# The opening of a fused attention kernel: query part before later keys, and a new planned order

## The chip, the cores and the metric

The kernel runs on one core of a Trainium2 chip. The metric is the device time of one execution in microseconds (us), the median of several; lower is better. Before the change it is 843.43 us, the median of 3 runs (843.15 to 843.75).

## The reference

Three layers run one after the other. Cut to what matters:

```python
# q, k, v: [4, 8, 1152, 64]; w_in [512, 2048], w_out [2048, 512]
q_pool = q.reshape(B, H, S // 2, 2, D).mean(axis=3)          # 576 queries per head
scores = scale * q_pool @ k.T
attn = exp(scores - scores.max(-1)); attn /= attn.sum(-1) + 1e-9
x = (attn @ v).transpose(0, 2, 1, 3).reshape(2304, 512)
h = x @ w_in;  x = (h * cos(h)) @ w_out
# then eight small experts, fed and read through softmax weights of x @ phi
```

## The kernel before, in words

The attention takes the 32 heads two at a time: 16 pairs, which the code numbers `p`, and which the change's title calls units. Two heads of 64 rows share the 128 partitions. A pair has two halves `c` of 288 queries each, and each half has nine steps `t`, one for each 128 keys.

The softmax needs each row's maximum before the exponentials. It is found by a cheap first pass in bfloat16: a **round** (`round_`, L346) multiplies two blocks of 64 queries with 384 keys, and VectorE takes the maximum of each row (`reduce`, L349). A pair has 14 rounds, 8 for the first five query blocks and 6 for the other four. When the rounds of a group are reduced, TensorE turns the maxima (`by_head`, L356), VectorE takes the maximum over keys (`top`, L363 and L368), and ScalarE and VectorE write diagonal matrices `D` with the negated maxima (L382, L380).

A **step** then is: the scores in float32 (L463, L450), the subtraction of the maximum as one more product with `D` (L472), the exponential on ScalarE (L477), and the product with the values (L485). Rounds and scores share three banks of PSUM (`BANKS = 3`): a round gives its bank back when it is reduced, a score when its exponential is done. The exponentials are also added up, on VectorE, on GpSimd, and some by a DMA that adds into memory and is issued from GpSimd (L495, L497, L500); `ADD0` and `ADD1` hold one letter for each step of a half that says who adds it, a small letter for the DMA.

Nothing orders these operations by hand. `Plan` holds every operation with an estimated duration and a due time, simulates the engines' queues with these estimates, and writes the instructions in the order in which the simulation started them. The due times come from tables (`ROUNDS`, `FIRST_ROUNDS`, `DUES`) and the step length `P`. The tables set nothing but the order; on the chip each engine runs its instructions in that order and waits for semaphores.

The opening is special. For the first pair the queries come in three parts of 128, 192 and 256 columns, two rows of which are added into one (L284), the keys in three parts of 384; each part is also cast to bfloat16 (L287). While TensorE would idle, 16 **warm** products (L419, four matmuls each) run into a bank that nobody reads. The load of the first values (L277) is held back by a copy of one element on ScalarE (L271).

After the attention come the two large matmuls (L905), whose weights are decoded from 64-bit words by VectorE, ScalarE and GpSimd (L832 to L869, eight parts of them during the attention), and at the end the experts.

Of the kernel before, what the change touches and what calls it, by code (L numbers as in the profile page):

```python
# [25 lines left out]
class Plan:  # L26
# [3 lines left out]
    HOP = 0.08  # L30
    TAIL = {"P": 0.17, "A": 0.1, "V": 0.085, "G": 0.04}

# [5 lines left out]
    def op(self, due, eng, time, fn, after=(), new=(), uses=(), port=None, more=0.0, early=0.0, name=""):  # L38

        i = len(self.ops)
        for ring, size, key in new:
            self.sizes[ring], self.sizes_of[key] = size, ring
        for key in [k for _, _, k in new] + list(uses):
            self.users.setdefault(key, []).append(i)
        port = (eng == "G") if port is None else port
        self.ops.append((due, eng, time, fn, list(after), list(new), port, more, early, name))
        return i

    def order(self):
# [34 lines left out]
        for _ in range(len(ops)):  # L86
# [21 lines left out]
            for j in outs[i]:  # L108
                at[j] = max(at[j], free[eng] if eng == ops[j][1] == "P" else end[i] + self.HOP)
                left[j] -= 1  # L110
# [5 lines left out]
    def by_path(self, first, last, due, most):  # L116

        left = {last: 0.0}
        for i in range(last, first - 1, -1):
            if i in left:  # L120
# [4 lines left out]
                for d in o[4]:  # L125
                    p = self.ops[d]
                    wait = 0.0 if o[1] == p[1] == "P" else self.HOP + self.TAIL.get(p[1], 0.0) + p[7]
                    left[d] = max(left.get(d, 0.0), left[i] + wait)
# [7 lines left out]
class Attention:  # L136
# [7 lines left out]

    P = 1.277
    QB, KC = 64, 384

    FIRST_ADD0 = "VVvGGVVGG"  # L150
    FIRST_ADD1 = "VGVgVVGVG"
    FIRST_JOIN_BY = "G"
    ADD0 = "VVGvgVVGG"
    ADD1 = "VVgvVGVGG"

    ROUNDS = (-7.4, -5.0, -18.6, -10.7, -8.1, -10.2, -3.5, -2.9, -10.5, 8.1, 1.5, 8.0, -1.0, 9.4)
    FIRST_ROUNDS = (-90, -89, -88, -87, -86, -85, -84, -83, -65.3, -9.1, -12.9, 5.0, -3.2, 3.6)
    E_BUFS = 10
    XU, AG = 5, 3
    SINGLE = (15,)  # L160
    ISSUE, LANDING = 0.95, 5.5

    BEHIND = 28.96

    DUES = {
        "load": 9.4, "free": -20.1, "v": 32.8, "pooled": 21.9, "qb": -10.3, "kb": -18.8, "top": -82.8,
        "diagonal": 52.5, "add": 39.2, "whole": -54.1, "take": -45.0, "join": -44.3, "sums": 15.4, "out": 18.1,
        "fold": -30.9, "inv": -20.5, "row": 39.3, "spread": 11.1, "scale": -3.8, "high": 72.8, "low": 25.6,
        "delta": 13.2,
    }  # L170
    CHAIN, DELTA_BY = (0, 2, 4, 7, 8), "V"
    JOIN_BY, SCALE_BY, LOW_BY = "V", "G", "G"

    BANKS = 3

    AHEAD = 3

    WARM_FROM, WARM, WARM_EVERY = 8.6, 16, 0.34

# [58 lines left out]
    def operands(self, p, m):  # L238
        nc, op = self.nc, self.plan.op
        J, NQ, KC, NC, QB = self.J, self.NQ, self.KC, self.NC, self.QB  # L240
        S = J * 128
        q, k = self.q[2 * p:2 * p + 2].rearrange("h d (r s) -> (h d) r s", r=2), self.k[2 * p:2 * p + 2]
        k = k.rearrange("h d s -> (h d) s")
        at_ = lambda name, n=0.0: m + self.DUES[name] * self.P + n
        early = 0.0 if p == 0 else max(at_("free"), 9.0)
        at = lambda parts: [(sum(parts[:i]), n) for i, n in enumerate(parts)]
        q_parts = at([QB * 2, QB * (self.half - 2), NQ - QB * self.half] if p == 0 else [NQ])
        k_parts = at([KC] * NC if p == 0 else [S])

        def tiles():  # L250
            if p == 0:
                self.qr[p] = self.one.tile([128, 2, NQ], FP32, name="qr")
            self.kr[p] = self.three.tile([128, S], FP32, tag="kr", name="kr")
            self.mp[p] = self.three.tile([128, sum(len(x) for x in self.rounds), 2], FP32, tag="mp", name="mp")
            self.qs[p] = self.three.tile([128, NQ], FP32, tag="qs", name="qs")
            self.qb[p] = self.two.tile([128, NQ], BF16, tag="qb", name="qb")
            self.kb[p] = self.two.tile([128, S], BF16, tag="kb", name="kb")

        def load_q(a, n):
            if p:  # L260
                nc.sync.dma_start(out=self.qs[p][:, a:a + n], in_=q[:, 0, a:a + n])
            else:
                nc.sync.dma_start(out=self.qr[p][:, :, a:a + n], in_=q[:, :, a:a + n])

        def load_k(a, n):
            (nc.sync if p or a else nc.scalar).dma_start(out=self.kr[p][:, a:a + n], in_=k[:, a:a + n])

        def values():
            self.vr[p] = self.late.tile([128, 2, J, 64], FP32, tag="vr", name="vr")
            if p == 0:  # L270
                nc.scalar.copy(out=self.vr[p][:, 0, 0, 0:1], in_=self.qs[p][:, 2 * QB:2 * QB + 1])  # L271

        def load_v():
            if p:
                values()
            vr = self.vr[p]
            nc.sync.dma_start(out=vr, in_=self.v[2 * p:2 * p + 2].rearrange("h p (j d) -> p h j d", d=64))  # L277

        def pooled(a, n):
            if p:  # L280
                nc.gpsimd.dma_start(out=self.qs[p][:, a:a + n], in_=q[:, 1, a:a + n], accum_op=ALU.add)
                return
            qr, x = self.qr[p], slice(a, a + n)
            nc.vector.tensor_tensor(out=self.qs[p][:, x], in0=qr[:, 0, x], in1=qr[:, 1, x], op=ALU.add)  # L284

        def copy(dst, src, a, n):
            nc.scalar.copy(out=dst[p][:, a:a + n], in_=src[p][:, a:a + n])  # L287

        ring = lambda names, size: [(n, size, (n, p)) for n in names]
        new = ring(["kr", "qs", "mp"], 3) + ring(["qb", "kb"], 2)  # L290
        first = op(m, "SP", 0.0, tiles, new=new, early=early)
        self.q_after[p], self.k_after[p], self.s_after[p] = {}, {}, []
        late = 0.0
        for i, (a, n) in enumerate(q_parts):
            x = op(m + 0.5 * i, "SP", 0.6, lambda a=a, n=n: load_q(a, n), [first], uses=[("qs", p)],
                   more=4.2 if p else (3.0, 3.7, 3.9)[i], early=early)
            if p:
                x = op(at_("pooled"), "G", self.ISSUE, lambda a=a, n=n: pooled(a, n), [x], uses=[("qs", p)], port=False, more=self.LANDING)
            else:
                x = op(m + (-40.0, -40.0, 40.0)[i] * (p == 0), "V", 0.07 + n / 960, lambda a=a, n=n: pooled(a, n), [x], uses=[("qs", p)], port=True)  # L300
            self.s_after[p].append(x)
            self.last_q[p] = x
            c = op(at_("qb", 0.1 * i) if p else m + 1.0 + i, "A", 0.07 + n / 1180, lambda a=a, n=n: copy(self.qb, self.qs, a, n), [x],
                   uses=[("qs", p), ("qb", p)])
            for y in range(0, NQ, QB):
                if a <= y < a + n:
                    self.q_after[p][y // QB] = [c]
        for i, (a, n) in enumerate(k_parts):
            x = op(m + (0.1, 0.2, 0.3)[i], "A" if p == 0 and i == 0 else "SP", 0.6, lambda a=a, n=n: load_k(a, n), [first], uses=[("kr", p)],
                   more=5.6 if p else (2.8, 3.2, 3.4)[i], early=early)  # L310
            self.s_after[p].append(x)
            for y in range(a, a + n, KC):
                self.k_after[p][y // KC] = [op(at_("kb", 0.1 * i) if p else m + 1.1 + i + y / 1e4, "A", 0.405, lambda y=y: copy(self.kb, self.kr, y, KC), [x],
                                               uses=[("kr", p), ("kb", p)])]
        if p:
            n = 128 * (len(self.CHAIN) - 1)

            def delta():
                x = self.kr[p]
                self.engine(self.DELTA_BY).tensor_tensor(out=x[:, 0:n], in0=x[:, 0:n], in1=x[:, 128:128 + n], op=ALU.subtract)  # L320

            x = op(at_("delta"), self.DELTA_BY, (0.07 + n / 960, 0.08 + n / 447)[self.DELTA_BY == "G"], delta,
                   sum([x for x in self.k_after[p].values()], []), uses=[("kr", p)], port=True, name="delta")
            self.delta_after[p] = [x]
        new, uses, x = [("vr", 2, ("vr", p))], [], [self.v_after[p - 1]] if p else []
        if p == 0:
            x = [op(m + 2.5, "A", 0.1, values, self.q_after[0][2], new=new, uses=[("qs", p)])]
            new, uses = [], [("vr", p)]
        self.v_after[p] = op(at_("v"), "SP", 0.6, load_v, x, new=new, uses=uses, more=4.2, early=early + late)


    def maximum(self, p):
        nc, plan, P = self.nc, self.plan, self.P
        st, reds = {}, []
# [413 lines left out]
FIRST = [(i, f) for i in range(4) for f in range(2)]  # L748

FIRST_AT = 12.0  # L750
FIRST_FROM, FIRST_EVERY, FIRST_DUE = 0.53, -0.08, 1000
SEL_C = 4
URGENT = 14.0, 12.0

# [897 lines left out]
```

## Time and profile before

| | |
|---|---|
| median of the runs | 843.43 us |
| the profiled execution | 844.42 us, its span 842.6 us |
| TensorE busy | 828.3 us (98%) |
| VectorE busy | 700.7 us (83%) |
| ScalarE busy | 524.9 us (62%) |
| GpSimd busy | 388.9 us (46%) |
| granted TensorE clock, mean | 0.995 |

All durations below are those of the profiled execution. A row of the timeline names its start, its duration, the engine, the line of the code, the output and the input, how many instructions it merges, and in brackets the idle time before it with what ended it. The durations of matmuls overlap, so the time that one costs is read from the start of the next.

### The profile page before, as it was taken

How to read it: one execution, taken by the hardware profiler on the slowest of the kernel's cores; microseconds unless marked ns; L12 is line 12 of the kernel's file. 1: busy time of each engine (PE TensorE's matmuls, PEld its weight loads, DVE VectorE, ACT ScalarE, POOL GpSimd, SP SyncE). 2: the span in 40 equal slices, each digit the busy share in tenths (PEclk: the TensorE clock that was granted, in tenths of full speed). 3: DMA queues.
4: the chain of work that ended last, by engine and by line, in shares of the span. 5: the costliest groups of instructions: out<-in, count | busy, mean ns of one | idle time of the engine just before them, and what ended most of it. 6: DMA issues, size and time to landing. Idle time of an engine off the chain costs nothing.

```text
span 842.6 us, 23109 instructions
## 1 busy us (share of the span) xinstructions
PE 828.3 (98%) x9439; PEld 610.8 (72%) x9439; DVE 700.7 (83%) x1291; ACT 524.9 (62%) x1118; POOL 388.9 (46%) x398
## 2 busy tenths in 40 slices
PE   6999999999999999999999999999999999999996
PEld 3666666666666666668888888888888888877456
DVE  7899999999999999858999898989899989544523
ACT  4777777777777777766875555555555555454223
POOL 1567666666667666674544334344443333120100
PEclk9999999999999999999999999999999999999998
DMA  7246555555555554221211111111111110693997
GB/s 238 45 114 144 132 132 143 132 138 125 141 126 129 131 132 90 50 69 38 63 50 38 39 51 38 42 50 41 49 38 51 38 39 13 243 422 142 358 422 238
DMA packets 48347, 99.30 MB, mean 118 GB/s; under 512 B 12144, under 2 KB 20336, under 8 KB 44144
## 3 DMA queue, kind: packets, MB, share of 16 engines
q1 hardware_dynamic: 41616, 84.35, 30.8%
q0 software_dynamic: 6480, 13.27, 9.5%
q8 instruction: 74, 1.21, 0.6%
q14 instruction: 33, 0.27, 0.1%
q10 hardware_dynamic: 144, 0.20, 0.1%
HBM read 78.71 MB, written 4.72 MB: 99 GB/s over the span
## 4 chain that ended last, share of the span: by engine, by line
PE 96%; POOL 1%; DVE 1%; ACT 1%; DMA 0%; issue 0%; SPq 0%; ACTq 0%; POOLq 0%
PE hps L905 23%; PE ops L905 23%; PE o L485 16%; PE s L463 10%; PE s L450 7%; PE m L346 4%; PE s L472 2%; PE so L1517 2%; PE hq L1474 2%; PE xtp L1086 1%; PE sums L619 1%; PE fo L1546 1%; DVE mp L349 1%; PE lgp L1100 1%; PE sps L1285 1%; PE lg L1109 0%
## 5 line engine op out<-in xcount | busy, mean ns | idle before, releaser
L349 DVE TENSOR_REDUCE mp<-m 128x2 f32<-128x768 f32 x224 | 206.2, 951 | 18.4 <-PE m L346 16.6
L477 ACT ACTIVATE e<-s 128x576 f32<-128x576 f32 x288 | 174.0, 650 | 54.7 <-PE s L450 23.6
L905 PE MATMUL ops<-w,g 128*128 128x512 f32 x864 | 205.5, 391 | 0.0
L905 PE MATMUL hps<-x,w 128*128 128x512 f32 (+1 forms) x960 | 204.4, 368 | 0.0
L905 PEld LDWEIGHTS hps<-x,w 128*128 128x128 f32 x960 | 167.9, 188 | 32.1 <-issue 1.7
L905 PEld LDWEIGHTS ops<-w,g 128*128 128x128 f32 x864 | 160.8, 188 | 33.6 <-issue 0.8
L485 PE MATMUL o<-e,vr 64*64 64x288 f32 x2304 | 177.3, 403 | 0.0
L943 POOL TENSOR_TENSOR g<-r,g 128x512 fp32r<-128x512 f32 (+1 forms) x80 | 100.2, 1253 | 145.3 <-ACT g L940 119.3
L930 ACT ACTIVATE r<-r 128x512 f32<-128x512 f32 (+1 forms) x160 | 94.0, 587 | 69.7 <-DVE r L923 68.0
L463 PE MATMUL s<-qs,kr 64*64 64x288 f32 x1344 | 110.5, 408 | 1.4 <-PE m L346 0.8
L497 POOL TENSOR_TENSOR acc<-acc,e 128x576 f32<-128x576 f32 x64 | 92.1, 1439 | 30.8 <-ACT e L477 28.8
L485 PEld LDWEIGHTS o<-e,vr 64*64 64x64 f32 x2304 | 86.9, 133 | 26.0 <-issue 0.4
L866 POOL TENSOR_TENSOR da<-da,w 128x256 f32<-128x256 f32 x64 | 51.4, 803 | 97.8 <-DVE db L855 42.0
L346 PE MATMUL m<-kb,qb 64*64 64x384 bf16 x896 | 75.7, 330 | 6.2 <-ACT qb L287 4.2
L450 PE MATMUL s<-qs,kr 64*64 64x288 f32 x960 | 80.1, 403 | 0.0
L923 DVE SCALAR_TENSOR_TENSOR r<-ki,hps 128x512 f32<-128x512 int32 (+1 forms) x80 | 50.4, 629 | 34.0 <-ACT ki L920 32.0
L940 ACT CAST g<-r 128x512 fp32r<-128x512 f32 (+1 forms) x80 | 46.2, 577 | 39.1 <-DVE r L933 36.6
L463 PEld LDWEIGHTS s<-qs,kr 64*64 64x64 f32 x1344 | 46.4, 132 | 31.7 <-ACT e L477 8.0
L920 ACT ACTIVATE ki<-hps 128x512 int32<-128x512 f32 (+1 forms) x80 | 44.0, 549 | 36.4 <-PE hps L905 35.3
L1066 DVE TENSOR_TENSOR acc<-acc,ops 128x512 f32<-128x512 f32 x70 | 47.6, 684 | 22.1 <-PE ops L905 22.0
L495 POOL DMA_DIRECT2D acc<-e x30 | 26.0, 868 | 86.3 <-ACT e L477 86.3
L346 PEld LDWEIGHTS <-qb 64*64 64x64 bf16 x896 | 34.4, 107 | 28.8 <-issue 4.6
(162 smaller groups left out, 1094.6 us busy)
## 6 DMA issues: line engine op xcount, KB each, us to landing
raw<-in_w_io_dram SPq DMA_DIRECT2D x64, 256.0 KB
w1t<-in_w_dram SPq DMA_DIRECT2D x15, 1024.0 KB
vr<-in_v_dram SPq DMA_DIRECT2D x16, 576.0 KB
kr<-in_k_dram SPq DMA_DIRECT2D x15, 576.0 KB
acc<-e POOLq DMA_DIRECT2D x30, 288.0 KB, 4.4
w2t<-in_w2b_dram SPq DMA_DIRECT2D x8, 1024.0 KB
qs<-in_q_dram SPq DMA_DIRECT2D x15, 288.0 KB
qs<-in_q_dram POOLq DMA_DIRECT2D x15, 288.0 KB, 4.5
```

The lines of the kernel that those rows point to most:

```text
L346: nc.tensor.matmul(ps[heads[c], h.start // 64, 0:self.KC], w, m, start=True, stop=True)
L349: nc.vector.tensor_reduce(out=self.mp[p][:, x], in_=st[i][:, :, 0:self.KC], axis=AX.X, op=ALU.max)
L450: nc.tensor.matmul(out, w, self.qs[p][x, s], start=False, stop=True, skip_group_check=True)
L463: nc.tensor.matmul(ps[y:y + 64, h, 0:N], w, self.qs[p][x, s], start=True, stop=False)
L477: nc.scalar.activation(out=st["e"], in_=st["ps"][:, :, 0:N], func=ACTF.Exp, scale=1.0 / 16.0)
L485: nc.tensor.matmul(self.o[u][64 * h:64 * h + 64, r, 0:N], self.vr[p][x, h, block(t)], st["e"][x, h], start=(t == 0), stop=(t == J - 1),)
L497: self.engine(who).tensor_tensor(out=acc[who], in0=x, in1=st["e"], op=ALU.add)
L866: nc.gpsimd.tensor_tensor(out=st["a"], in0=st["a"], in1=fl(half(0)), op=ALU.subtract)
L905: nc.tensor.matmul(ps, x, y, start=(i == 0 and m == 0), stop=(i == n - 1 and m == 2))
L923: nc.vector.scalar_tensor_tensor(out=st["r"], in0=st["ki"], scalar=-c, in1=x, op0=ALU.mult, op1=ALU.add)
L930: nc.scalar.activation(out=st["r"], in_=st["r"], **kw)
L943: nc.gpsimd.tensor_tensor(out=g["l"][:, i], in0=st["r"], in1=fl(g["h"][:, i]), op=ALU.subtract)
```

## The change

The second part of the first pair's queries is loaded before the second and third parts of its keys; the third part is still loaded last. Its planned landing times are new. The third part's add on VectorE gets an earliest planned time, which puts it behind the first diagonals. The copy that holds back the values' load waits for the cast of the last keys too. Two steps of some halves change hands: from the third pair on, the DMA adds step 2 of a second half instead of step 3, and in the first halves of the first two pairs step 3 instead of step 2 (`ADD0` names other letters for the same adds). `AHEAD`, the number of scores that may stand before the diagonals, goes from 3 to 1. All due times are new.

```diff
-    P = 1.277
+    P = 1.282
-    FIRST_ADD0 = "VVvGGVVGG"
+    FIRST_ADD0 = "VVgvGVVGG"
-    ADD0 = "VVGvgVVGG"
-    ADD1 = "VVgvVGVGG"
+    ADD0 = "VVgvgVVGG"
+    ADD1 = "VVvgVgVGG"
...
-    FIRST_ROUNDS = (-90, -89, -88, -87, -86, -85, -84, -83, -65.3, -9.1, -12.9, 5.0, -3.2, 3.6)
+    FIRST_ROUNDS = (-90, -89, -88, -87, -86, -85, -84, -83, -56.3, 4.6, -13.0, -6.0, 3.8, 4.6)
...
-    AHEAD = 3
+    AHEAD = 1
...
-            x = op(m + 0.5 * i, "SP", 0.6, lambda a=a, n=n: load_q(a, n), [first], uses=[("qs", p)],
-                   more=4.2 if p else (3.0, 3.7, 3.9)[i], early=early)
+            x = op(m + (0.0, 0.05, 0.9)[i], "SP", 0.6 if p else 0.45, lambda a=a, n=n: load_q(a, n), [first], uses=[("qs", p)],
+                   more=4.2 if p else (3.0, 3.3, 4.0)[i], early=early)
...
-                x = op(m + (-40.0, -40.0, 40.0)[i] * (p == 0), "V", 0.07 + n / 960, lambda a=a, n=n: pooled(a, n), [x], uses=[("qs", p)], port=True)
+                x = op(m + (-40.0, -40.0, 40.0)[i] * (p == 0), "V", 0.07 + n / 960, lambda a=a, n=n: pooled(a, n), [x], uses=[("qs", p)], port=True, early=12.7 * (i == 2))
...
-            x = [op(m + 2.5, "A", 0.1, values, self.q_after[0][2], new=new, uses=[("qs", p)])]
+            x = [op(m + 5.0, "A", 0.1, values, self.q_after[0][2] + self.k_after[0][2], new=new, uses=[("qs", p)])]
...
-FIRST_FROM, FIRST_EVERY, FIRST_DUE = 0.53, -0.08, 1000
+FIRST_FROM, FIRST_EVERY, FIRST_DUE = 1.25, -0.46, 1000
```

Every engine has the same instructions as before, and behind the first few pairs they stand in the same order. What moves is the start. On the queue of the loads (SP), at the head of the program, `qr` is the raw queries, `kr` the keys and `vr` the values:

```order
 L263 DMA qr<-in_q_dram 128x2x128
+L263 DMA qr<-in_q_dram 128x2x192
 L266 DMA kr<-in_k_dram 128x384 x2
-L263 DMA qr<-in_q_dram 128x2x192
 L263 DMA qr<-in_q_dram 128x2x256
 L277 DMA vr<-in_v_dram 128x2x576
```

The second part of the queries has moved past the two loads of keys.

On VectorE, in the opening of the first pair, `qs<-qr` is the add of a query part, `mp<-m` the reduce of a round, `mc` the maximum over keys and `D` a diagonal:

```order
 L224 TENSOR_SCALAR a_minus<-ident 64x64 x2
 L284 TENSOR_TENSOR qs<-qr 128x128
-L349 TENSOR_REDUCE mp<-m 128x2 x2
 L284 TENSOR_TENSOR qs<-qr 128x192
-L349 TENSOR_REDUCE mp<-m 128x2
+L349 TENSOR_REDUCE mp<-m 128x2 x8
+L363 TENSOR_REDUCE mc<-m 128x2x2
+L368 TENSOR_REDUCE mc<-m 128x1
+L380 TENSOR_SCALAR D<-a_minus,mc 128x64 x2
 L284 TENSOR_TENSOR qs<-qr 128x256
-L349 TENSOR_REDUCE mp<-m 128x2 x6
-L363 TENSOR_REDUCE mc<-m 128x2x2
```

The second add now stands before the first reduce, the third behind the diagonals, and eight reduces instead of nine stand before the maximum over keys.

On GpSimd, in the second half of a later pair, the numbers tell exponentials apart: `e_1440` is step 3, which ScalarE computes before step 2, `e_1453`. Before:

```order
L281 DMA qs_1325<-in_q_dram 128x576
L495 DMA acc_1451<-e_1440 128x576
L497 TENSOR_TENSOR acc_1485<-e_1453,e_1465 128x576
L497 TENSOR_TENSOR acc_1485<-acc_1485,e_1520 128x576
L497 TENSOR_TENSOR acc_1485<-acc_1485,e_1570 128x576
```

Now:

```order
L281 DMA qs_1325<-in_q_dram 128x576
L495 DMA acc_1451<-e_1453 128x576
L497 TENSOR_TENSOR acc_1485<-e_1440,e_1465 128x576
L497 TENSOR_TENSOR acc_1485<-acc_1485,e_1520 128x576
L497 TENSOR_TENSOR acc_1485<-acc_1485,e_1570 128x576
```

The two exponentials have changed places; the order of the instructions is the same.

On TensorE the 16 warm products keep their number and change their places: before, 12 of them stand in front of the turning of the first maxima (L356) and 4 between it and the first subtraction (L472), with three rounds among those 4; now 9 stand in front and 7 between, with no round among them.

## Rows read from the trace of the kernel before

**Rows 1.** The page's chain that ended last, by engine.

```profile
PE 96%; POOL 1%; DVE 1%; ACT 1%; DMA 0%; issue 0%; SPq 0%; ACTq 0%; POOLq 0%
```

**Rows 2.** Windows: stretch, length, busy of five engines (instructions), clock, DMA share, GB/s.

```profile
10.00:20.00 10.00, 8.57 (x156) 5.30 (x155) 9.19 (x16) 4.00 (x10) 1.01 (x1) 1.00 1.00 327
100.00:200.00 100.00, 99.99 (x1884) 66.59 (x1880) 94.56 (x145) 77.26 (x171) 63.65 (x63) 1.00 0.55 132
```

**Rows 3.** Timeline of the queue of the loads: late query parts, first values.

```profile
2.59 1.22 SPq L263 DMA_DIRECT2D qr<-in_q_dram  x2
...
8.06 0.39 SPq L277 DMA_DIRECT2D vr<-in_v_dram  x1
```

**Rows 4.** Timeline of the opening, VectorE and ScalarE.

```profile
4.82 0.96 DVE L349 TENSOR_REDUCE mp<-m 128x2 f32<-128x768 f32 x1 [0.97 <-PE m L346]
...
5.19 1.09 ACT L287 CAST kb<-kr 128x384 bf16<-128x384 f32 x2 [1.01 <-DMA kr<-in_k_dram]
...
7.21 0.35 DVE L284 TENSOR_TENSOR qs<-qr 128x192 f32<-128x192 f32 x1
...
12.14 2.69 DVE L349 TENSOR_REDUCE mp<-m 128x2 f32<-128x768 f32 x3 [0.19 <-PE m L346]
```

**Rows 5.** Timeline of the opening, TensorE.

```profile
4.23 0.53 PE L346 MATMUL m<-kb,qb 64*64 64x384 bf16 x4 [4.23 <-ACT qb L287]
...
7.66 1.24 PE L463 MATMUL s<-qs,kr 64*64 64x288 f32 x8 [0.80 <-PE m L346]
...
8.65 0.90 PE L346 MATMUL m<-kb,qb 64*64 64x384 bf16 x8
...
9.29 0.90 PE L419 MATMUL o<-kb,qb 64*64 64x384 bf16 x8
```

**Rows 6.** Timeline around the turning of the maxima, first half and second half.

```profile
14.12 0.30 PE L356 MATMUL m<-mp,ident 64*64 64x8 f32 x8
...
14.75 0.16 DVE L363 TENSOR_REDUCE mc<-m 128x4 f32<-128x12 f32 x1
...
14.94 0.82 ACT L382 ACTIVATE D<-a_minus,mc 128x64 bf16<-128x64 f32 x3 [5.74 <-DVE mc L363]
...
22.52 0.24 PE L356 MATMUL m<-mp,ident 64*64 64x6 f32 x8
...
22.84 0.17 DVE L363 TENSOR_REDUCE mc<-m 128x4 f32<-128x12 f32 x1 [0.65 <-PE m L356]
```

**Rows 7.** Timeline of TensorE from the first subtraction on.

```profile
16.30 0.36 PE L346 MATMUL m<-kb,qb 64*64 64x384 bf16 x4 [0.57 <-DVE mp L349]
16.46 0.32 PE L472 MATMUL s<-D,a_ones 64*64 64x288 bf16 x4
17.17 0.72 PE L463 MATMUL s<-qs,kr 64*64 64x288 f32 x8 [0.39 <-DVE mp L349]
...
17.82 0.67 PE L463 MATMUL s<-qs,kr 64*64 64x288 f32 x8
...
19.04 0.67 PE L485 MATMUL o<-e,vr 64*64 64x288 f32 x8
```

**Rows 8.** Timeline of later pairs: exponentials, GpSimd's adds, and VectorE beside them.

```profile
95.81 2.96 ACT L477 ACTIVATE e<-s 128x576 f32<-128x576 f32 x5 [0.33 <-PE s L472]
...
98.50 0.86 POOL L495 DMA_DIRECT2D acc<-e  x1 [2.09 <-ACT e L477]
...
100.90 0.68 DVE L320 TENSOR_TENSOR kr<-kr 128x512 f32<-128x512 f32 x1
...
116.77 1.41 POOL L497 TENSOR_TENSOR acc<-acc,e 128x576 f32<-128x576 f32 x1
...
117.61 1.19 DVE L497 TENSOR_TENSOR acc<-acc,e 128x576 f32<-128x576 f32 x1
```

**Rows 9.** Timeline of TensorE: row sums of the first pair and of the fourth.

```profile
50.24 0.70 PE L619 MATMUL sums<-acc,a_ones 128*32 128x144 f32 x16
...
116.26 0.70 PE L619 MATMUL sums<-acc,a_ones 128*32 128x144 f32 x16
```

More of the change, by code (lines that the diff above doesn't have):

```diff
@@ L136 @@
 class Attention:
-    P = 1.277
+    P = 1.282
     QB, KC = 64, 384
-    FIRST_ADD0 = "VVvGGVVGG"
+    FIRST_ADD0 = "VVgvGVVGG"
     FIRST_ADD1 = "VGVgVVGVG"
     FIRST_JOIN_BY = "G"
-    ADD0 = "VVGvgVVGG"
-    ADD1 = "VVgvVGVGG"
-    ROUNDS = (-7.4, -5.0, -18.6, -10.7, -8.1, -10.2, -3.5, -2.9, -10.5, 8.1, 1.5, 8.0, -1.0, 9.4)
-    FIRST_ROUNDS = (-90, -89, -88, -87, -86, -85, -84, -83, -65.3, -9.1, -12.9, 5.0, -3.2, 3.6)
+    ADD0 = "VVgvgVVGG"
+    ADD1 = "VVvgVgVGG"
+    ROUNDS = (-8.3, -4.7, -20.1, -9.5, -8.3, -10.2, -3.6, -2.8, -10.1, 0.8, -0.0, 0.5, 7.4, 9.2)
+    FIRST_ROUNDS = (-90, -89, -88, -87, -86, -85, -84, -83, -56.3, 4.6, -13.0, -6.0, 3.8, 4.6)
     E_BUFS = 10
@@ L161 @@
     ISSUE, LANDING = 0.95, 5.5
-    BEHIND = 28.96
+    BEHIND = 28.21
     DUES = {
[L166 to L169, printed above, removed]
+        "load": 16.1, "free": -31.4, "v": 39.2, "pooled": 27.6, "qb": 2.7, "kb": -27.1, "top": -88.5,
+        "diagonal": 39.2, "add": 48.0, "whole": -54.3, "take": -58.3, "join": -53.6, "sums": 15.1, "out": 16.7,
+        "fold": -29.6, "inv": -41.6, "row": 24.2, "spread": 20.3, "scale": -5.7, "high": 74.6, "low": 36.3,
+        "delta": 20.0,
     }
@@ L308, in operands @@
         for i, (a, n) in enumerate(k_parts):
-            x = op(m + (0.1, 0.2, 0.3)[i], "A" if p == 0 and i == 0 else "SP", 0.6, lambda a=a, n=n: load_k(a, n), [first], uses=[("kr", p)],
-                   more=5.6 if p else (2.8, 3.2, 3.4)[i], early=early)
+            x = op(m + (0.1, 0.2, 0.3)[i], "A" if p == 0 and i == 0 else "SP", 0.6 if p else 0.45, lambda a=a, n=n: load_k(a, n), [first], uses=[("kr", p)],
+                   more=5.6 if p else (2.6, 3.4, 3.7)[i], early=early)
             self.s_after[p].append(x)
```

## The prediction

> **What bounds the kernel now.** I read the chain of waits first: it is TensorE for 96% of the span [rows 1]. The windows then say where TensorE is not full. In a hundred microseconds of the attention it is busy for 99.99 of 100 us, while VectorE has 94.56 [rows 2]. From the row sums of the first pair to those of the fourth there are 66.02 us, 22.0 us a pair [rows 9], and in that stretch TensorE is fed without gaps. In the opening it is not: from 10 to 20 us it is busy for 8.57 us [rows 2], and much of that is warm products and matmuls at half speed. So the end of the kernel moves by what the opening wins or loses, as long as TensorE stays full behind it. Both programs have the same products on TensorE before the first row sums at 50.24 us. So one question remains: how much of those 50 us TensorE spends on nothing useful.
>
> What ends last in the opening is VectorE's eight reduces, then the turning of the maxima (14.12 us), the diagonals and the first subtraction at 16.46 us [rows 6, 7]. That first subtraction, here called X, is the mark for which I work out a new time.
>
> **When the reduces run.** Before, the first reduce starts at 4.82 us and the second query part is added at 7.21 us only, so the rounds of blocks 2 to 4 come late [rows 4]; its load was issued with the third from 2.59 us on, behind the keys [rows 3]. Now it has the place of the second key part, which has the same 192 KB and landed for the cast at 5.19 us [rows 4]. I take 5.2 us for its landing, the row of the same size and place. Its bounds are 4.2 us (the first part is there by 3.6, since its round starts at 4.23 [rows 5] after an add and a cast; 192 KB at the 327 GB/s of [rows 2] are 0.6 us more) and 7.2 us, when the add ran before [rows 4]. Each microsecond above 6.1 would reach the end, as the next part shows; below, it is covered by TensorE. The add takes 0.35 us [rows 4] and now stands ahead of the first reduce, which starts at about 5.5 us, 0.7 us later than before. The cast of that part then ends near 5.9 us (under 0.5 us, the length of a cast of keys in [rows 4]), and a round's matmuls need 0.59 us until the reduce starts (4.23 to 4.82 [rows 4, 5]), so the second reduce starts at 6.5 us. From there they run back to back, 0.90 us each (2.69 us for three [rows 4]): the eighth ends at 6.5 + 6 x 0.9 + 0.96 = 12.9 us. Before, nine reduces ended at 12.14 + 2.69 = 14.83 us. On VectorE alone that is a gain of 1.9 us, of which 0.9 is the ninth reduce that now waits.
>
> **When TensorE is ready.** It must do, after the bank of the fourth reduce comes free (6.5 + 2 x 0.9 + 0.96 = 9.3 us), the seventh and the eighth round, nine warm products, and a score. In the rows of the opening such a group of four bfloat16 matmuls takes 0.32 us (8.65 to 9.29 for two) and a score 0.99 us (7.66 to 8.65) [rows 5]. Later they take 0.16 (16.30 to 16.46) and about half a microsecond [rows 7]. The granted-clock column reads 1.00 from 10 to 20 us [rows 2], but the spacing says that the opening runs at 1.2 GHz and goes to 2.4 GHz between those rows, after TensorE had been packed from 7.66 us on. Now it is packed later, from 9.3 us on. At half speed the list takes 11 x 0.32 + 0.99 = 4.5 us, and the turning starts at 13.8 us instead of 12.95. I take 13.8.
>
> The Trainium skill, "TensorE: Matmul & The Clock Gate", Part 1, says that the throttled state is the default, that activity releases it, and that the point of release shifts from run to run. The trace agrees with the first two: half speed in [rows 5], full speed in [rows 7]. No run here shows the third. By that rule a sparser opening would get its clock later, which speaks against this change; the rival below prices it.
>
> **From the turning to X.** Before, VectorE was in its ninth reduce when the maxima were turned. With VectorE free, the maximum over keys starts 0.32 us after the turning (22.52 to 22.84), the diagonals 0.19 us later (14.75 to 14.94) and take 0.82 us [rows 6]: X can start at 13.8 + 0.32 + 0.19 + 0.82 + 0.07 = 15.2 us. In front of it TensorE has seven warm products. At full speed they take 7 x 0.16 = 1.1 us and are hidden; at half speed 2.2 us, and X starts at 16.1. Before, X stood behind three rounds, of which the last waited 0.57 us for a bank [rows 7]; that wait is gone. So X moves from 16.46 to 15.2 us: **1.26 us gained**.
>
> **What is given back.** Before, 12 rounds were done when X started, now 8. TensorE still has to do the four: 4 x 0.16 = **0.65 us lost**. One score stands ahead of X in both orders, so `AHEAD` by itself costs nothing.
>
> Behind X, before, the next score waited for a bank: 17.17 - 16.46 - 0.12 = 0.59 us [rows 7]. Now that bank is free, but the six rounds of the second half all come behind X. The first can start 0.73 us after X (a subtraction and a step of 0.65, 17.17 to 17.82 [rows 7]); the next bank comes free with the first exponential, 0.2 us late. Six reduces and the keys' difference (0.68 [rows 8]) keep VectorE busy until about 1.15 + 5.4 + 0.7 = 7.3 us behind X, and TensorE wants to turn the second maxima at 6.7 us. That is 0.2 + 0.6 = 0.8 us of waits against 0.59: **0.2 us lost**. Its bounds are -0.6 (no wait at all) and +1.0 (each of the six rounds waits 0.27 us).
>
> **Edits that I cost at nothing.** The third query part's add and cast come after the diagonals; they are hidden behind the first two products after X, and if that cover went, the first exponential would start up to 0.4 us later, a cast's length. The values' load is released by the last key cast instead of a query cast; it went out at 8.06 us and its first use is at 19.04 [rows 3, 7], so a microsecond either way is covered. Behind it on SP stand the second pair's loads, and the decoded weights' words now stand behind the second values; ScalarE wants them only behind the first two exponentials and the next pair's key casts, so some microseconds are spare; if they were late, the exponentials behind them on ScalarE would wait as long.
>
> The exchange of steps 2 and 3 comes back in each of the last 14 pairs. The DMA now waits for the fourth of five exponentials that take 2.96 us from 95.81, so it can go at about 98.2 us plus its start; it went at 98.50 [rows 8]. It and the add behind it are 0 to 0.6 us later. An add on GpSimd that runs beside one of VectorE's can hold it: one that started at 117.61 took 1.19 us, while GpSimd added from 116.77 to 118.18, so at most 0.57 us of it were a hold [rows 8]. If the difference of keys at 100.90 is held by 0.15 us in every pair, and TensorE with it, that is 14 x 0.15 = 2.1 us; if the shift takes a hold away, the same is won. VectorE is full for 94.56 of 100 us [rows 2], not 100, so I take nothing.
>
> The Trainium skill, "SBUF — State Buffer", section "Who interferes with whom", says that a VectorE instruction with two inputs in SBUF and a GpSimd instruction that reads SBUF exclude each other for the whole instruction. The 1.19 us row agrees. By that rule the later GpSimd add would run into the keys' difference, with the 2.1 us above.
>
> **The sum.** -1.26 + 0.65 + 0.2 = -0.4 us. The profiled execution took 844.42 us, of which 842.6 are span; it would take 844.0. The median of the runs is 0.99 us below it, 843.43, and goes to **843.0 us**.
>
> **Rivals.**
>
> *The clock comes later (slower).* Its place is the seven warm products and the score ahead of X. If full speed comes only after 15 us, X starts at 16.1: 0.35 gained, 0.65 and 0.2 lost, so 843.9 us. It decides from the point where X is later than 15.6. For it: TensorE starts to be packed 1.6 us later than before (9.3 against 7.66). Against it: the half-speed rounds before that are work too.
>
> *The clock comes early and VectorE sets X.* If full speed comes by 12 us, the turning starts at 12.95 and X at 14.35: 2.1 gained, 0.65 lost, and without new waits behind X 0.6 more won: 841.4 us. For it: before, full speed came no later than 14 us. Against it: the packed stretch starts late.
>
> *The exchange of the steps costs the later pairs (slower).* 2.1 us as above, less 0.4: 845.1 us, with a bit more if the DMA's sum also comes late for VectorE's next add. Against it: the order on all engines is the same there.
>
> *The change does nothing:* the opening ends where it ended, 843.4. That is inside the forecast's own range.
>
> **How the numbers follow.** The forecast, with its neighbours within 1 us, gets 0.58; the late clock 0.15; the early clock 0.15; the exchange 0.07; 0.05 for what I don't see, on either side. 0.2% is 1.7 us, about what a measurement of this kernel can tell from no change: faster means under 841.7, slower over 845.1. The early clock at 841.4 reaches faster with most of its chance, and part of the unseen joins it: 0.18. Slower needs the exchange at its full price or more: 0.08. The rest, 0.74, is no change. The range from 841.2 to 844.7 takes in both clocks and a score's wait more or less, and leaves out the full price of the exchange and the far ends.
>
> **What would show it.** In the changed profile: the second query part's add near 5.2 us; the eighth reduce ending near 12.9; the turning at 13 to 14; X at 15.2; no wait of a score behind X but waits of rounds; the first row sums at 49.8 instead of 50.24; and 22.0 us a pair behind them. The prediction is wrong in its main step if X is later than 16 us or earlier than 14.4, and in its frame if the distance between row sums changes.

## The result: slower by 0.6%, and the profile after

The changed kernel took 849.53 us in the median of six runs (847.96 to 852.03), the kernel before 843.71 in six runs beside it (843.15 to 844.69): a ratio of 1.0062, with an interval of 1.0051 to 1.0074. That is outside the range of 841.2 to 844.7. The profiled execution is the fastest of the six, 847.96 us with a span of 846.2, so its span lies only 3.6 us above the 842.6 of the profile before, where the medians are 5.8 us apart.

In the opening, the chain of steps came as predicted, each a little later. The timeline of the changed kernel, the queue of the loads, VectorE, ScalarE and TensorE, from the first load to the first row sums:

```profile
0.74 1.35 SPq L263 DMA_DIRECT2D qr<-in_q_dram  x2
...
5.67 0.36 DVE L284 TENSOR_TENSOR qs<-qr 128x192 f32<-128x192 f32 x1 [1.80 <-DMA qr<-in_q_dram]
5.95 0.95 DVE L349 TENSOR_REDUCE mp<-m 128x2 f32<-128x768 f32 x1
7.06 6.15 DVE L349 TENSOR_REDUCE mp<-m 128x2 f32<-128x768 f32 x7 [0.16 <-PE m L346]
7.36 0.38 SPq L277 DMA_DIRECT2D vr<-in_v_dram  x1
...
14.23 0.33 PE L356 MATMUL m<-mp,ident 64*64 64x8 f32 x8
14.38 1.34 PE L419 MATMUL o<-kb,qb 64*64 64x384 bf16 x28
...
14.83 0.82 ACT L382 ACTIVATE D<-a_minus,mc 128x64 bf16<-128x64 f32 x3 [7.50 <-DVE mc L363]
15.71 0.32 PE L472 MATMUL s<-D,a_ones 64*64 64x288 bf16 x4
...
54.76 0.70 PE L619 MATMUL sums<-acc,a_ones 128*32 128x144 f32 x16
```

The second query part is added at 5.67 us (predicted 5.2), the eighth reduce ends at 13.21 (12.9), the maxima are turned at 14.23 (13.8), and X starts at 15.71 (15.2), 0.75 us earlier than before [rows 7]. But the first row sums come at 54.76 us, 4.52 us later than before [rows 9]. Behind them no more is lost. The row sums of the fourth pair come at 121.12, 66.36 us behind the first, against 66.02; but from the first row sums to the last ones of L619 it is 302.30 us, against 302.68 before. The rows, two of the changed kernel and one of the kernel before:

```profile
121.12 0.70 PE L619 MATMUL sums<-acc,a_ones 128*32 128x144 f32 x16
...
357.06 0.70 PE L619 MATMUL sums<-acc,a_ones 128*32 128x144 f32 x16
```

```profile
352.92 0.70 PE L619 MATMUL sums<-acc,a_ones 128*32 128x144 f32 x16
```

So the loss lies between X and 54.76. The page's chain by engine and the windows of the changed kernel show on which engines:

```profile
PE 93%; DVE 3%; DMA 1%; ACT 1%; POOL 1%; issue 0%; SPq 0%; DVEq 0%; ACTq 0%; POOLq 0%
```

```profile
10.00:20.00 10.00, 9.98 (x165) 6.73 (x161) 7.31 (x13) 5.06 (x12) 1.02 (x1) 1.00 1.02 336
20.00:30.00 10.00, 9.57 (x180) 5.86 (x172) 9.87 (x16) 7.21 (x17) 5.97 (x5) 1.00 0.38 73
30.00:40.00 10.00, 9.18 (x176) 6.06 (x180) 9.42 (x16) 6.83 (x16) 5.37 (x4) 1.00 0.11 21
40.00:50.00 10.00, 7.47 (x139) 4.53 (x132) 10.00 (x11) 5.82 (x11) 5.69 (x6) 1.00 0.57 141
```

VectorE has 3% of the chain where it had 1% [rows 1]. From 10 to 20 us TensorE is fuller than before (9.98 against 8.57 us, [rows 2]); from 20 to 50 us it is idle for 0.43 + 0.82 + 2.53 = 3.78 us, and VectorE is full or nearly so (9.87, 9.42 and 10.00 of 10 us). What VectorE does there stands in the groups of instructions by line from 16 to 56 us, first of the changed kernel, then of the kernel before (16 to 51.5 us); behind the bar stand the busy time in us and the mean ns of one:

```profile
L850 DVE SCALAR_TENSOR_TENSOR da<-raw,da 128x256 int32<-128x256 int32 x2 | 5.6, 2787 | 0.0
```

```profile
L850 DVE SCALAR_TENSOR_TENSOR da<-raw,da 128x256 int32<-128x256 int32 x2 | 0.8, 420 | 0.0
```

Two instructions of the weights' decode, in which the sign is set (the sign step), take 4.8 us more. The timeline of the changed kernel around them, VectorE, GpSimd and the round on TensorE that waits:

```profile
27.88 1.70 POOL L497 TENSOR_TENSOR acc<-acc,e 128x576 f32<-128x576 f32 x1
27.88 1.99 DVE L850 SCALAR_TENSOR_TENSOR da<-raw,da 128x256 int32<-128x256 int32 x1
...
45.16 3.58 DVE L850 SCALAR_TENSOR_TENSOR da<-raw,da 128x256 int32<-128x256 int32 x1
45.41 1.69 POOL L500 TENSOR_TENSOR acc<-acc 128x576 f32<-128x576 f32 x1
46.78 1.67 POOL L497 TENSOR_TENSOR acc<-e 128x576 f32<-128x576 f32 x1
...
49.66 0.36 PE L346 MATMUL m<-kb,qb 64*64 64x384 bf16 x4 [2.53 <-DVE mp L349]
```

Each sign step ends 0.3 us after GpSimd's adds beside it: the first after one add (29.58), the second after two without a pause (48.45). The reduces behind it start as much later, and TensorE waits for a bank. Before, both sign steps ran together at 24.27 us, when GpSimd was idle; the lines of the kernel before, the two steps and GpSimd's next add with the idle time ahead of it:

```profile
24.27 0.76 DVE L850 SCALAR_TENSOR_TENSOR da<-raw,da 128x256 int32<-128x256 int32 x2
...
25.56 1.41 POOL L497 TENSOR_TENSOR acc<-acc,e 128x576 f32<-128x576 f32 x1 [2.39 <-ACT e L477]
```

The planner's new tables moved the steps; which of the tables did it, no run separates. Beside the three GpSimd instructions at 43.4 to 47 us VectorE ran reduces before the change. They read PSUM, and they kept their 0.92 us.

`Plan` does know of such meetings: operations marked `port=True`, GpSimd's adds and VectorE's sign step among them, never overlap in its simulated time. But it hands on only an order for each engine, and on the chip both sign steps met adds.

### The profile page after: what moved, and what is told of

It is laid out like the page before. It is cut to its first block, busy times and chain, and to the rows that moved or that the text cites. A ratio compares the mean times of both kernels' runs of the same rounds, so it can differ in the third digit from the quotient of the medians.

```text
span 846.2 us, 23100 instructions
## 1 busy us (share of the span) xinstructions
PE 828.4 (98%) x9439; PEld 609.6 (72%) x9439; DVE 704.1 (83%) x1291; ACT 525.5 (62%) x1118; POOL 389.9 (46%) x398
## 4 chain that ended last, share of the span: by engine, by line
PE 93%; DVE 3%; DMA 1%; ACT 1%; POOL 1%; issue 0%; SPq 0%; DVEq 0%; ACTq 0%; POOLq 0%
PE hps L905 23%; PE ops L905 23%; PE o L485 15%; PE s L463 9%; PE s L450 6%; PE m L346 4%; PE s L472 2%; PE so L1517 2%; PE hq L1474 2%; DVE mp L349 1%; PE sums L619 1%; PE xtp L1086 1%; PE fo L1546 1%; DVE da L850 1%; PE lgp L1100 1%; DMA fold<-r 1%
## 5 line engine op out<-in xcount | busy, mean ns | idle before, releaser
L497 POOL TENSOR_TENSOR acc<-e 128x576 f32<-128x576 f32 x32 | 54.0, 1687 | 12.1 <-ACT e L477 12.1
```

Of the source, the lines that this page charges most:

```text
L497: self.engine(who).tensor_tensor(out=acc[who], in0=x, in1=st["e"], op=ALU.add)
```

## Experiments

I set three theories against each other. **Theory 1**: the sign steps wait for GpSimd's adds, and these two waits (here called holds) are the loss. **Theory 2**: VectorE starts later behind X with all six rounds of the second half before it, and would be the bound with any order. **Theory 3**: another edit costs it, above all the order of the loads. The orders were edited behind the planner, by a table of moves that is applied to the finished list (name of an operation, and the one behind which it goes). `sign(1, 3)` is the first sign step, `sign(0, 3)` the second; `reduce2.4` is the reduce of round 4 for `p` = 2. `high(0, 3)` is the cast on ScalarE (L863) that reads what the second sign step wrote, so it has to move with that step.

**Both steps moved.**

```diff
+    MOVES = (("sign(1, 3)", "reduce1.4"), ("sign(0, 3)", "reduce2.4"), ("high(0, 3)", "diagonal1.1"))
-        todo = sorted(range(len(ops)), key=lambda i: (start[i], ops[i][0], i))
+        todo = self.arranged(sorted(range(len(ops)), key=lambda i: (start[i], ops[i][0], i)), ops)
```

> The changed kernel with two VectorE instructions later in its row: the sign step of the first decoded weight part (line 850) two reduces later, that of the second behind the six reduces of its stretch and one more; the same instructions in all. Theory 1 (VectorE is held while a two-input step of the decode stands beside GpSimd's adds, 1.99 and 3.58 us instead of 0.42): both steps take under 0.6 us, the first row sums come at 49.8 to 50.5 us instead of 54.76, and the time is 842.8 to 844 us. Theory 2 (VectorE starts late behind the first subtraction, is the bound for the first pair and would be late with any order): the row sums stay later than 53 us and the time at 847 or above.

Measured: 844.66 us (11 runs) against 844.20 of before on that chip, ratio 1.0003 (0.9995 to 1.0012). Its timeline, VectorE and TensorE:

```profile
29.62 0.42 DVE L850 SCALAR_TENSOR_TENSOR da<-raw,da 128x256 int32<-128x256 int32 x1
...
50.22 0.41 DVE L850 SCALAR_TENSOR_TENSOR da<-raw,da 128x256 int32<-128x256 int32 x1
...
50.23 0.70 PE L619 MATMUL sums<-acc,a_ones 128*32 128x144 f32 x16
...
53.45 1.50 DVE L855 TENSOR_SCALAR db<-da 128x256 int32<-128x256 int32 x1
```

Two VectorE instructions in another place, with the cast behind one of them, and the whole loss is gone. Theory 2 falls: VectorE has the same work behind an X that is no later (15.39 us here). This run also bears on theory 3: it keeps every other edit of the change and takes the time of before, so all the others together cost nothing that shows. The median lies 0.7 us above the expected band and cannot be told from before.

**One step moved.** The first entry alone, then the other two:

```diff
+    MOVES = (("sign(1, 3)", "reduce1.4"),)
...
+    MOVES = (("sign(0, 3)", "reduce2.4"), ("high(0, 3)", "diagonal1.1"))
```

> The changed kernel with the first of the two sign steps alone moved two reduces later. Theory 1: the hold of 1.99 us goes and gives 1 to 1.6 us back, row sums near 53.4, time 846 to 848.5; the second step is still held for 2 to 3.6 us. Theory 2: no change of the row sums beyond 0.4 us.

> The changed kernel with the second of the two sign steps alone moved behind the reduces. Theory 1: the hold of 3.58 us goes and gives 2.3 to 3.2 us back, row sums near 52, time 845 to 847; the first step is still held for 1 to 2 us. Theory 2: no change of the row sums beyond 0.4 us.

Measured: 849.23 us with the first moved (1.0059, 1.0046 to 1.0072), 846.65 with the second moved (1.0031, 1.0018 to 1.0043). The second came as expected: its row sums are at 51.59, the first step is still held for 1.99 us. The first did not: its row sums came at 54.98, later than in the changed kernel. Its timeline and windows show why:

```profile
43.89 3.58 DVE L850 SCALAR_TENSOR_TENSOR da<-raw,da 128x256 int32<-128x256 int32 x1
...
48.39 0.54 PE L346 MATMUL m<-kb,qb 64*64 64x384 bf16 x4 [2.53 <-DVE mp L349]
48.66 1.22 PE L485 MATMUL o<-e,vr 64*64 64x288 f32 x8
```

```profile
46.00:48.00 2.00, 0.00 (x0) 0.00 (x0) 2.00 (x2) 0.50 (x2) 1.17 (x1) 1.00 1.00 229
48.00:50.00 2.00, 1.61 (x16) 1.10 (x19) 2.00 (x3) 0.45 (x1) 1.40 (x1) 0.51 1.04 368
50.00:52.00 2.00, 2.00 (x28) 1.32 (x24) 0.85 (x2) 0.65 (x1) 0.30 (x1) 0.63 0.13 53
```

The second hold came 1.27 us earlier, as it should. But behind TensorE's idle time the granted clock is 0.51 in one window of 2 us: TensorE works at the lower of its two levels, 1.2 GHz instead of 2.4, and a product with the values takes 1.22 us instead of 0.68. In the next window it is 0.63 in the mean, and behind that 1.00. In the changed kernel the same 2.53 us of idle time left the clock at 1.00 (the round at 49.66 takes 0.36 us, here 0.54). In this profile, what was won was lost to the clock: (1 - 0.51) x 1.61 + (1 - 0.63) x 2.00 = 1.5 us, an estimate from the two windows. Only this one of its five runs has a trace.

**The step done again in the kernel before.** Nothing of the change is in these three. In the first, `sign(0, 3)` is done a second time beside GpSimd's adds (its result is the same); in the second, the same repetition stands where GpSimd pauses; in the third, the step at L855, with one input in SBUF, is repeated at the place of the first.

```diff
+    AGAIN = (("sign(0, 3)", "reduce2.5"),)
...
+    AGAIN = (("sign(0, 3)", "reduce1.10"),)
...
+    AGAIN = (("power(0, 3)", "reduce2.5"),)
```

> The kernel before with one instruction more: the sign step of a decoded part (line 850, 0.42 us) is done a second time on VectorE, among the six reduces at 43.9 to 49.4 us, while GpSimd does three adds without a pause (43.4 to 47 us). Theory 1 (a two-input step waits for GpSimd's adds, all of a row without a pause): the added step takes 1 to 3.6 us instead of 0.42, the first row sums come 1 to 3.5 us later than 50.24 and the time is 1 to 3.5 us above before. Theory 2 (VectorE is merely late or full): 0.42 us for the step and at most 0.5 us in the time.

> The same added sign step in the kernel before, some reduces earlier, where GpSimd has nothing to do (38.7 to 43.4 us). Both theories: the step takes 0.42 us, and the time is 0 to 0.5 us above before. Where theory 1 holds, this run and the one with the step beside the adds differ by 1 to 3 us though they have the same instructions.

> The kernel before with one instruction more at the very place where the repeated sign step was held: instead of it the step at line 855, which reads one tensor from SBUF instead of two and takes 0.29 us, is done a second time among the six reduces, beside GpSimd's three adds. If only a step with two inputs waits for GpSimd: 0.29 us, and the time within 0.5 us of before. If any VectorE instruction that works on SBUF alone waits (one row of the changed kernel has this step at 1.50 us beside an add): 1 to 3.5 us for the step, the row sums later than 51 us, and 1 to 5 us in the time. The reduces, which read PSUM, keep 0.9 us each by both.

Measured: 849.03 us beside the adds (1.0056, 1.0042 to 1.0069) and 843.63 in the pause (0.9997, 0.9988 to 1.0006), against 843.91 of before; 849.71 with one input beside the adds, against 844.20 (1.0061, 1.0047 to 1.0075). The timeline of the first, VectorE, GpSimd and TensorE, and its windows:

```profile
45.32 1.63 POOL L497 TENSOR_TENSOR acc<-e 128x576 f32<-128x576 f32 x1
45.63 3.63 DVE L850 SCALAR_TENSOR_TENSOR da<-raw,da 128x256 int32<-128x256 int32 x1
46.72 0.91 POOL L866 TENSOR_TENSOR da<-da,w 128x256 f32<-128x256 f32 x1
47.40 1.57 POOL L497 TENSOR_TENSOR acc<-acc,e 128x576 f32<-128x576 f32 x1
...
50.18 0.54 PE L346 MATMUL m<-kb,qb 64*64 64x384 bf16 x4 [3.21 <-DVE mp L349]
...
55.10 0.70 PE L619 MATMUL sums<-acc,a_ones 128*32 128x144 f32 x16
```

```profile
50.00:52.00 2.00, 1.82 (x20) 1.24 (x23) 1.86 (x3) 0.00 (x0) 2.00 (x3) 0.52 0.00 0
52.00:54.00 2.00, 2.00 (x32) 1.29 (x31) 0.96 (x1) 0.00 (x0) 0.23 (x1) 0.63 0.58 72
```

The second, in the pause, and the third, with one input, in their timelines:

```profile
39.62 0.41 DVE L850 SCALAR_TENSOR_TENSOR da<-raw,da 128x256 int32<-128x256 int32 x1
...
50.36 0.70 PE L619 MATMUL sums<-acc,a_ones 128*32 128x144 f32 x16
```

```profile
45.84 3.50 DVE L855 TENSOR_SCALAR db<-da 128x256 int32<-128x256 int32 x1
```

One instruction of 0.42 us costs 5 us at one place and nothing at another. The step waits through three GpSimd instructions, TensorE waits 3.21 us, and the clock is at its lower level behind that; the price exceeds the expected 1 to 3.5 us by the clock. Behind the last row sums (358.01 us beside the adds, 352.64 in the pause) these two programs take the same: 847.3 - 358.01 = 489.3 us and 841.9 - 352.64 = 489.3. The number of inputs does not matter here: the step with one input takes 3.50 us where it takes 0.29 alone. No run moves GpSimd's adds and leaves the step; that the adds hold it rests on the place, and on each of these long steps ending 0.2 to 0.3 us after the last of them.

**The order of the loads alone**, in the kernel before:

```diff
+    MOVES = (("q0.1", "q0.0"), ("pool0.1", "pool0.0"), ("cast0.1", "cast0.0"))
```

> The kernel before with the first part of the change alone: the second query part is loaded ahead of the later keys, and its add on VectorE and its cast on ScalarE stand where its landing puts them; the rounds, the warm products and all else stay in the order of before. Theory 1 (the loss comes from the two sign steps alone): no sign step is held, the first row sums within 0.7 us of 50.24, the time within 0.8 us of before. Theory 3 (the order of the loads itself costs): the second and third key parts land late, the rounds wait, the row sums come 1 us late or more, and so does the end.

Measured: 844.27 us against 843.91, ratio 1.0002 (0.9993 to 1.0010); row sums at 50.19. Theory 3 falls for the loads: by themselves, with the add and the cast of the part that was moved, they cost and win nothing that shows. X comes at 16.41 us there, behind the same wait of 0.57 us for a reduce [rows 7].

**Can the opening win?** In the run of both moves X is 1.07 us earlier than before, and the row sums are no earlier. I therefore moved X further: seven of the 16 warm products into TensorE's idle time before 9.3 us, 6 left between there and the turning instead of 9, 3 behind it instead of 7, and the second score ahead of X. (Here the table gives the number of warm products behind each operation, and the line below it puts the second score behind the turning.) The next run also loads the second pair's queries in the place of the first pair's third query part.

```diff
+    AGAIN = (("round0.0", 4), ("round0.3", 1), ("round0.4", 1), ("round0.5", 1), ("round0.6", 2), ("round0.7", 3), ("first score", 1), ("second score", 3))
+        todo.insert(next(n for n, i in enumerate(todo) if ops[i][9] == "turn0.0") + 1, len(ops) - 1)
...
+    MOVES = (..., ("tiles1", "k0.2"), ("q1.0", "tiles1"), ("q0.2", "v0"))
```

> The changed kernel with both sign steps moved as in the run of both moves, and the opening of TensorE arranged by what its trace shows: seven of the 16 warm products stand in the idle time between the first rounds (4.7 to 9.3 us), four instead of ... seven in the half-speed stretch before the turning are fewer, and the second score stands ahead of the first subtraction instead of behind it. If TensorE's half-speed list is what sets the turning (eighth reduce at 12.7, turning at 13.7 us): turning near 12.8, first subtraction at 14.2 to 14.8 instead of 15.4, first row sums near 49 instead of 50.23, and 842.5 to 843.7 us against 844.66 of the run of both moves. If the clock comes as much later: no difference to that run.

> The run with the arranged opening, with one exchange on the queue of the loads more: the second pair's queries are loaded in the place of the first pair's third query part, which is needed at 14 us only and goes out behind the first values. In the arranged opening TensorE started the first subtraction at 14.6 us instead of 15.4 and then stood 1.06 us at 23.5 for the cast of the second pair's queries, which landed at 22.2 us. If that landing is the next bound: the cast starts before 20 us, the wait at 23.5 us is gone, the row sums come at 49.2 to 49.7 instead of 50.48, and the time is 0.8 to 1.3 us under that run, 842.8 to 843.4. If VectorE or something else is the bound behind it: row sums at 50 us or later, no difference to the run without the exchange.

Measured: 844.30 us against 843.91 (1.0008, 0.9996 to 1.0020), and 843.76 against 844.20 (0.9999, 0.9989 to 1.0008). The timeline of the first, TensorE and ScalarE:

```profile
13.16 0.30 PE L356 MATMUL m<-mp,ident 64*64 64x8 f32 x8 [0.94 <-DVE mp L349]
...
14.60 0.44 PE L472 MATMUL s<-D,a_ones 64*64 64x288 bf16 x8
...
22.26 0.67 ACT L287 CAST qb<-qs 128x576 bf16<-128x576 f32 x1 [2.21 <-DMA qs<-in_q_dram]
...
23.53 0.36 PE L346 MATMUL m<-kb,qb 64*64 64x384 bf16 x4 [1.06 <-ACT e L477]
```

X is at 14.60, yet the row sums come at 50.48, not near the expected 49. The second pair's queries land at 22.2 us, no earlier than in the changed kernel (where their cast starts at 22.33), and TensorE stands for 1.06 us until the exponential behind their cast on ScalarE is done. With their load moved the cast starts at 20.67, that wait is gone, and the row sums come at 49.85, 0.39 earlier than before. Of the 1.87 us won at X in this second run (14.59), 0.65 are the rounds still to be done and 0.71 stand in three waits of TensorE until 19.1 us (0.28, 0.19 and 0.24); the rest stays open. In the time neither version can be told from the kernel before, so both expectations of a gain failed.

**The changed kernel again**, with nothing edited, for the spread of its runs.

> The changed kernel once more, unchanged. Its six runs lay between 847.96 and 852.03 us, those of before between 843.15 and 844.69. Theory 1: how long a sign step is held hangs on where in GpSimd's adds it starts, so the two steps at line 850 take other times in this profile than 1.99 and 3.58 us, and the span differs by about as much; outside these rows the two profiles agree. Theory 2: the steps take the same time and the spread comes from elsewhere, such as the clock of the opening (first subtraction not at 15.7 us).

Measured: 850.77 us (850.10 to 851.33). The steps are held as long as in the first profile (2.00 and 3.58 us) and the row sums come at 54.58, so theory 1 is wrong about the spread. Against the first profile this execution lost its 2.8 us later: 2.0 between the first and the last row sums (304.30 us against 302.30) and 1.0 behind them, less the 0.2 us by which the first come earlier. Between the row sums of the third and the fourth pair there are 121.77 - 98.67 = 23.10 us, against 21.95 in the first profile; there TensorE waits 1.1 us for a reduce. Between the fifth and the sixth there are 166.53 - 143.72 = 22.81, against 22.17, and 22.50 in the kernel before; no wait of a microsecond is seen there. Why executions differ in such pairs stays open. The holds explain the 4.5 us at the first row sums, in both profiles; what the changed kernel loses in some executions beyond that they do not explain by themselves.

## Why the prediction was wrong

The step that failed is the frame: "So the end of the kernel moves by what the opening wins or loses, as long as TensorE stays full behind it." I worked out the opening and did not ask what VectorE does beside GpSimd between X and the first row sums. The decode's moves were among the edits costed at nothing, with their loads and ScalarE as cover; the two sign steps on VectorE have no cover. VectorE is nearly full there, so a hold goes through the next reduces and their banks to TensorE. Where the sum has nothing for them, the runs showed 1.57 + 3.16 = 4.7 us of holds, 4.52 us at the first row sums, and the time of before once the two steps stood elsewhere.

- *Reduces, turning, X*: right in kind, 0.3 to 0.5 us late in the profiled run. The -1.26 us at X were -0.75; in the four runs with the same opening X came at 15.13 to 15.43.
- *Given back*: predicted 0.85 us. With the holds out of the way all of the 1.07 us at X was given back.
- *The hold by GpSimd*: I had the mechanism and put it in the wrong place. I looked for it in the exchange of the two steps, in the last 14 pairs, and sized it by the one row at hand, at most 0.57 us [rows 8]. It cost nothing there (302.30 us from the first to the last row sums against 302.68, and the run of both moves keeps the exchange at the time of before); it cost 1.57 and 3.16 us ahead of the first row sums. The row showed what was left of one add; the long holds here lasted until all the GpSimd instructions that stood without a pause were done.
- *Clock*: neither early nor late clock in the opening decided anything: in the run with X at 14.60 us a round's four matmuls take 0.16 us from 9.6 us on (9.61 to the next start at 9.77), where in the changed kernel such a group still takes 0.32 at 10.71, and the time was that of before. The clock mattered behind the hold, where I had not looked for it.

The chance of slower, 0.08, was far too small: it hung on one mechanism at one place, while the change had moved every due time of the decode.

## What to carry to other kernels

When a planner's tables change, compare on VectorE and GpSimd what now stands beside what, for every instruction that works on SBUF alone, before the gain is worked out. Here a short VectorE step was dear beside a row of GpSimd adds (5 us in the time) and free in GpSimd's pause, while reduces from PSUM beside the same adds kept their time. A hold is not dear by itself: in the run of both moves L855 takes 1.50 us beside an add at 53.45 us, TensorE is busy all the while, and the time is that of before. It was dear where TensorE then stood and waited for the reduces behind it. A gain at the start of a pipeline is worth no more than what stands behind it allows: here 1.87 us at X became 0.39 at the first row sums, and nothing that shows in the time.

## What the runs showed of the hardware

A VectorE step on SBUF beside GpSimd's adds was not served between two GpSimd instructions: in the run with the step repeated beside the adds it took 3.63 us, until 0.29 us after the third of them, though the second and the third started 1.1 and 1.8 us after it. The Trainium skill, "SBUF — State Buffer", section "Who interferes with whom", says that the engine that issues first has the shared ports for its whole instruction and that the other is blocked. The first add fits that, the two behind it do not, as far as the starts in the trace tell. Nor does the second hold of the changed kernel: the step starts at 45.16 us, 0.25 us before the first of the two adds, and waits for both. Here the measurement decides.

The same section of the Trainium skill says that VectorE's operations with a scalar can, under conditions, take both pairs of ports with a single input, and then contend as well. The 3.50 us of the step with one input agrees.

After TensorE stood still for 2.53 to 3.21 us, the granted clock was at or near its lower level in three profiles (0.51 to 0.53 in the first 2 us with work), came back in the next 2 us (0.61 to 0.63 in the mean), and stayed at 1.00 in the two of the changed kernel, after 2.53 and 2.54 us. It cost these three profiles about 1.5 to 1.6 us more, an estimate from the windows: in the repeated step beside the adds (1 - 0.52) x 1.82 + (1 - 0.63) x 2.00 = 1.6 us of busy time at full speed. Why it fell in some and not in others the runs do not show.
